# A new order for the last seven-product block, and its last output tile sent in quarters

One NeuronCore of one Trainium2 chip runs the kernel. The metric is device time in microseconds (us), the slowest core's; there is only one core here.

## The reference

A linear attention with decay over blocks of 64 tokens, followed by a two-layer perceptron with a tanh GELU. Cut to what matters:

```python
def _attn_setup():
    batch, n_heads, seq, head_dim = (4, 8, 768, 64)
...
    x = attn_out.transpose(0, 2, 1, 3).reshape(B * S, H * D)      # 3072 x 512
...
def _moe_ref(x, w_in, w_out):                                     # w_in 512 x 2048, w_out 2048 x 512
    h = x @ w_in
    c = np.float32(np.sqrt(2.0 / np.pi))
    g = 0.5 * h * (1.0 + np.tanh(c * (h + 0.044715 * h * h * h)))
    return (g @ w_out).astype(np.float32)
```

The change touches only the very last part of `g @ w_out`.

## The kernel before

The 3072 tokens are worked through in groups; from the third group on a group has 512 tokens. The second matrix product of such a group is done with seven block products in place of eight (a Strassen scheme). The tokens form two halves of 256 (T = 0, 1), the output columns two halves of 256 (e = 0, 1). A "pair" p is 128 tokens of the upper half together with 128 of the lower; a group has two pairs, and each pair takes seven products of 8 matmuls. The results land in PSUM banks called A to E, and VectorE combines them into an output tile `o` with four quarters `o[:, e, T, :]`. Quarters with e = T are the diagonal.

```python
        banks = {}
        PLACE = {4: ("A", 0), 3: ("A", 1), 5: ("B", 0), 2: ("B", 1), 1: ("C", 0), 7: ("D", 0),
                 6: ("D", 1)}

        def product(m, p):
            name, half = PLACE[m]
            final = g == len(groups) - 1 and p == HN // P - 1
            if final and m == 6:
                name = "E"
            ...                                   # 8 matmuls into banks[name][:, half]
            if m == 2:                            # A and B are complete
                o = banks["o"] = otp.tile([P, 2, 2, HE], FP32, tag="o32", name="o32")
                ...                               # ScalarE copies B to m525 (L476, L477)
                pin(tt(banks["diag"], A[:], m525[:, 0:2], ALU.subtract))        # L480
                pin(tt(flat[:, 1:3], A[:], m525[:, 1:3], ALU.add))              # L481: off-diagonal, final
            elif m == 1:
                d = banks["diag"]
                pin(tt(d, banks["C"][:, 0].unsqueeze(1).to_broadcast([P, 2, HE]), d, ALU.add))   # L484
            elif final and m in (7, 6):
                ...
                if m == 7:
                    low = row0 + HN + p * P
                    pin(nc.sync.dma_start(out=out[low : low + P, 0:HE], in_=o[:, 0, 1, :]))      # L492
                d = o[:, T, T, :]
                pin(tt(d, banks[name][:, half], d, ALU.add))                    # L494
                if m == 7:
                    pin(nc.scalar.dma_start(out=rows, in_=o[:, :, 0, :]))       # L496: 256 KB
                else:
                    pin(nc.sync.dma_start(out=rows[:, 1], in_=d))               # L498: 128 KB
            elif m == 6:                          # every other pair
                ...                               # L501, then two transfers of 256 KB (L504)
        ...
        for p in range(HN // P):
            for m in (3, 4, 5, 2, 1, 7, 6):
                filler.append(lambda m=m, p=p: product(m, p))
```

`pin` keeps program order. In the last group nothing else is left to run beside these products.

Of the kernel before, what the change touches and what calls it, by code (L numbers as in the profile page):

```python
# [15 lines left out]
def kernel(  # L16
# [10 lines left out]
    nc = tc.nc  # L27
    pin = tc.keep_in_program_order
    P = 128
# [47 lines left out]
    HF, HE = NF // 2, DM // 2  # L77
# [302 lines left out]
    groups = [[0, 1], [2], [3], [4, 5], [6, 7], [8, 9], [10, 11]]  # L380
    group_of = {sb: (g, i) for g, sbs in enumerate(groups) for i, sb in enumerate(sbs)}
    filler = []

    def queue_group(g):
# [22 lines left out]
        row0 = groups[g][0] * SB  # L407
# [19 lines left out]
        HN = N // 2  # L427
# [7 lines left out]
        def block(T, F, i):  # L435
            return gT[:, i, F, T * HN : (T + 1) * HN]
# [8 lines left out]
                i = slice(i0, i1)  # L445
                pin(nc.vector.tensor_tensor(gsum[m][:, i, :], block(T0, F0, i), block(T1, F1, i), op))  # L446

        banks = {}
        PLACE = {4: ("A", 0), 3: ("A", 1), 5: ("B", 0), 2: ("B", 1), 1: ("C", 0), 7: ("D", 0),
                 6: ("D", 1)}  # L450

        def product(m, p):

            name, half = PLACE[m]
            final = g == len(groups) - 1 and p == HN // P - 1
            if final and m == 6:
                name = "E"
            if m in (3, 5, 1, 7) or name == "E":
                banks[name] = ps_M.tile([P, 2, HE], FP32, tag="M", name=f"M{name}")
            dst = banks[name][:, half]  # L460
            t = slice(p * P, p * P + P)
            for i in range(HF):
                lhsT = block(*G_PLAIN[m], i)[:, t] if m in G_PLAIN else gsum[m][:, i, t]
                if m in W_PLAIN:
                    F, E = W_PLAIN[m]
                    rhs = w_out16[:, F * HF + i, E * HE : E * HE + HE]
                else:
                    rhs = w_sum16[:, w_slot[m], i, :]
                pin(nc.tensor.matmul(dst, lhsT, rhs, start=(i == 0), stop=(i == HF - 1),  # L469
                                     skip_group_check=True))  # L470
            tt = nc.vector.tensor_tensor
            if m == 2:
                o = banks["o"] = otp.tile([P, 2, 2, HE], FP32, tag="o32", name="o32")
                A, B = banks["A"], banks["B"]
                m525 = mtp.tile([P, 3, HE], FP32, tag="m525", name="m525")
                pin(nc.scalar.activation(out=m525[:, 0:2], in_=B[:], func=AF.Copy))  # L476
                pin(nc.scalar.activation(out=m525[:, 2], in_=B[:, 0], func=AF.Copy))  # L477
                flat = o[:].rearrange("p e t d -> p (e t) d")
                banks["diag"] = flat[:, 0:4:3]
                pin(tt(banks["diag"], A[:], m525[:, 0:2], ALU.subtract))  # L480
                pin(tt(flat[:, 1:3], A[:], m525[:, 1:3], ALU.add))  # L481
            elif m == 1:
                d = banks["diag"]
                pin(tt(d, banks["C"][:, 0].unsqueeze(1).to_broadcast([P, 2, HE]), d, ALU.add))  # L484
            elif final and m in (7, 6):

                o, T = banks["o"], (0 if m == 7 else 1)
                row = row0 + T * HN + p * P
                rows = out[row : row + P, :].rearrange("q (e d) -> q e d", e=2)
                if m == 7:  # L490
                    low = row0 + HN + p * P
                    pin(nc.sync.dma_start(out=out[low : low + P, 0:HE], in_=o[:, 0, 1, :]))  # L492
                d = o[:, T, T, :]
                pin(tt(d, banks[name][:, half], d, ALU.add))  # L494
                if m == 7:
                    pin(nc.scalar.dma_start(out=rows, in_=o[:, :, 0, :]))  # L496
                else:
                    pin(nc.sync.dma_start(out=rows[:, 1], in_=d))  # L498
            elif m == 6:
                d = banks["diag"]  # L500
                pin(tt(d, banks["D"][:], d, ALU.add))  # L501
                for T in range(2):
                    row = row0 + T * HN + p * P
                    pin(nc.sync.dma_start(out=out[row : row + P, :].rearrange("q (e d) -> q e d", e=2),  # L504
                                          in_=banks["o"][:, :, T, :]))
# [16 lines left out]
        if g == 0:  # L522
# [9 lines left out]
            order = [(tau, part) for part in (0, 2, 1, 3) for tau in range(3)]  # L532
# [7 lines left out]
        if g == 1:  # L540
# [1 line left out]
                for part in (0, 2, 1, 3):  # L542
                    filler.append(lambda tau=tau, part=part: mm2(tau, part))
            return
        for p in range(HN // P):
            for m in (3, 4, 5, 2, 1, 7, 6):
                filler.append(lambda m=m, p=p: product(m, p))

        def behind(k, i0, i1):

# [28 lines left out]
    def R(n, s):  # L579
        if n is not None:  # L580
            scores(n)
        products(n, s)
        if n is not None:
            causal(n)
        if s is not None and s % 2 == 1:
            g, i = group_of[s // 2]
            if i == len(groups[g]) - 1 and g > 0:
                queue_group(g)
        if n is not None:
            update(n, 0)  # L590
# [41 lines left out]
    banks = products(3, None)  # L632
# [3 lines left out]
    cast_win(0, 256, 512, 256, c01, on_act=True)  # L636
    causal(3)
    queue_group(0)
    fill(4)
    products(None, 3, banks)  # L640
# [46 lines left out]
    for n in range(8, NSTEP + 1):  # L687
        m = n if n < NSTEP else None
# [42 lines left out]
```

## Time and profile before

| | before |
|---|---|
| time, median of 3 (range) | 207.87 us (207.51 to 208.07) |
| span of the profiled run | 205.60 us |
| TensorE busy | 96% |
| products of the last group | 188.34 to 200.58 us |
| last addition on VectorE starts | 200.95 us |
| last output transfer issued / landed | 201.39 / 204.05 us |

The page of a profile gives busy shares and the chain of work that ended last. A line of the timeline reads: start and length in us, engine and line of code, operation, output and inputs, count; a bracket at its end tells how long the engine stood idle before it and what ended that. SPq and ACTq are the queues on which SyncE and ScalarE issue transfers: the length there is that of the issue, not of the transfer. When packets moved and when each transfer landed is in the trace's own records; those I quote in the text.

### The profile page before, as it was taken

To read this page: it belongs to the slowest core of one execution; us is meant where nothing else is said; L and a number is where in the kernel's file an instruction comes from. 1 tells how busy PE (TensorE), PEld (TensorE's weight loads), DVE (VectorE), ACT (ScalarE), POOL (GpSimd) and SP (SyncE) were. 2 spreads that over 40 slices of the span, in tenths; PEclk is the share of its full clock that TensorE was granted. 3 is DMA by queue.
4 is the path that set the end of the run, shared out by engine and by line. 5 is a ranking of instruction groups with operands and counts; after the bars stand their busy time and mean duration, and the time that the engine had idled before them with its cause. 6 is when DMAs were issued, how large, how long until landed. Compare 5 with 4: busy or idle time off the path is not lost.

```text
span 205.6 us, 5583 instructions
## 1 busy us (share of the span) xinstructions
PE 197.1 (96%) x2321; PEld 128.0 (62%) x2321; DVE 144.4 (70%) x271; ACT 108.1 (53%) x204; POOL 69.9 (34%) x80
## 2 busy tenths in 40 slices
PE   7988999999999999999999999999999999999990
PEld 2554644456875788644788554788555888446880
DVE  4788627867699998929997639996559474056631
ACT  2355778475882573487541577442676323665110
POOL 5495123646586851326224403404420110000000
PEclk9999999999999999999999999999999999999999
DMA  5999999999999998996549981736320003300033
GB/s 137 298 322 387 387 387 376 277 291 332 333 248 243 294 235 154 202 279 161 141 102 274 230 234 50 190 70 156 103 54 0 3 0 105 104 0 0 3 102 102
DMA packets 64057, 37.85 MB, mean 184 GB/s; under 512 B 17696, under 2 KB 59168, under 8 KB 64032
## 3 DMA queue, kind: packets, MB, share of 16 engines
q1 hardware_dynamic: 63760, 37.24, 66.9%
q8 instruction: 18, 0.29, 0.6%
q10 hardware_dynamic: 272, 0.26, 0.4%
q14 instruction: 7, 0.06, 0.1%
HBM read 27.27 MB, written 6.29 MB: 163 GB/s over the span
## 4 chain that ended last, share of the span: by engine, by line
PE 91%; DVE 2%; DMA 2%; issue 1%; ACT 1%; DVEq 0%
PE Hps L401 35%; PE O2ps L416 10%; PE MB L469 8%; PE MA L469 7%; PE MD L469 7%; PE Sps L271 4%; PE MC L469 4%; PE Hps L514 4%; PE OK L329 3%; PE idle L573 3%; PE OK L320 3%; PE Tps L242 2%; DMA qkT<-qk 2%; PE OK L306 1%; DVE t L366 1%
## 5 line engine op out<-in xcount | busy, mean ns | idle before, releaser
L401 PE MATMUL Hps<-xT,w_in 128*128 128x512 f16 (+1 forms) x416 | 79.1, 346 | 0.0
L405 ACT ACTIVATE gT<-Hps 128x512 f16<-128x512 f32 x88 | 52.3, 597 | 22.6 <-PE Hps L401 21.8
L401 PEld LDWEIGHTS <-w_in 128*128 128x128 f16 x416 | 40.2, 98 | 33.5
L373 POOL TENSOR_TENSOR u<-t,lumask 128x256 f16<-128x256 f32 x40 | 31.4, 791 | 80.9 <-DVE t L366 54.2
L446 DVE TENSOR_TENSOR gs<-gT 128x512 f16<-128x512 f16 (+1 forms) x70 | 36.6, 586 | 10.8 <-ACT gT L405 10.6
L280 DVE TENSOR_TENSOR PT<-Sps,mask 128x1024 f16<-128x1024 f32 x24 | 29.2, 1217 | 17.3 <-PE Sps L271 17.2
L469 PEld LDWEIGHTS <-gs 128*128 128x128 f16 x360 | 34.9, 98 | 4.0
L211 POOL TENSOR_TENSOR v<-v,dv 128x512 f16<-128x512 f32 x24 | 29.2, 1219 | 4.7 <-DMA v<-in_v_dram 4.7
L343 ACT ACTIVATE xT<-OK 128x256 f16<-128x256 f32 x48 | 18.2, 453 | 20.0 <-PE OK L329 16.5
L416 PE MATMUL O2ps<-w_out,gT 128*128 128x512 f16 x96 | 21.9, 379 | 0.0
L476 ACT ACTIVATE m<-MB 128x512 f32<-128x512 f32 x9 | 5.4, 597 | 28.1 <-PE MB L469 28.1
L226 ACT ACTIVATE qk<-k 128x512 f16<-128x512 f32 x24 | 15.0, 624 | 8.8 <-DMA k<-in_k_dram 8.8
L221 DVE TENSOR_TENSOR qk<-q,dq 128x512 f16<-128x512 f32 x23 | 19.2, 834 | 0.0
L469 PE MATMUL MA<-w_sum,gT 128*128 128x256 f16 x144 | 17.5, 273 | 0.1
L469 PE MATMUL MD<-w_sum,gs 128*128 128x256 f16 x136 | 17.5, 273 | 0.0
L469 PE MATMUL MB<-w_out,gs 128*128 128x256 f16 x144 | 17.2, 273 | 0.0
L366 DVE SCALAR_TENSOR_TENSOR t<-t,lamu,OK 128x64 f32<-128x64 f32 x64 | 14.5, 273 | 2.1 <-PE OK L306 0.9
L480 DVE TENSOR_TENSOR o<-MA,m 128x512 f32<-128x512 f32 x9 | 6.2, 688 | 13.9 <-ACT m L476 13.9
L469 PEld LDWEIGHTS <-gT 128*128 128x128 f16 x144 | 14.0, 98 | 2.8 <-ACT gT L405 0.3
L416 PEld LDWEIGHTS <-gT 128*128 128x128 f16 x96 | 9.2, 98 | 9.9
L271 PEld LDWEIGHTS <-qkT 64*64 64x64 f16 x384 | 6.1, 106 | 8.3 <-issue 4.2
L123 DVE TENSOR_TENSOR w_sum<-wo,wo 128x1024 f16<-128x1024 f32 x6 | 7.9, 1362 | 4.2 <-DMA wo<-in_moe_w_out_dram 4.2
(55 smaller groups left out, 169.2 us busy)
## 6 DMA issues: line engine op xcount, KB each, us to landing
q<-in_q_dram SPq DMA_DIRECT2D x24, 256.0 KB, 4.5
k<-in_k_dram SPq DMA_DIRECT2D x24, 256.0 KB, 5.0
v<-in_v_dram SPq DMA_DIRECT2D x24, 256.0 KB, 4.9
out_dram<-o SPq DMA_DIRECT2D x22, 256.0 KB, 3.4
wo<-in_moe_w_out_dram SPq DMA_DIRECT2D x4, 1024.0 KB, 9.2
wi<-in_moe_w_in_dram SPq DMA_DIRECT2D x4, 512.0 KB, 8.0
wi<-in_moe_w_in_dram SPq DMA_DIRECT2D x2, 1024.0 KB, 12.5
out_dram<-o SPq DMA_DIRECT2D x2, 128.0 KB, 2.2
```

What stands on the lines that cost most here:

```text
L211: pin(nc.gpsimd.tensor_tensor(wide(tv[:]), ld32[s][2][:], decay(dv, s), ALU.mult))
L221: pin(q_eng.tensor_tensor(wide(tq), q32[:], decay(dq, s), ALU.mult))
L226: pin(nc.scalar.activation(out=wide(tk), in_=k32[:], func=AF.Copy))
L280: pin(nc.vector.tensor_tensor(t[:].rearrange("p a b c d -> p (a b) (c d)"), Ss.pop(n)[:].rearrange("p a b c d -> p (a b) (c d)"), mask[:]. ...
L343: pin(nc.scalar.activation(out=dst[:, :, c * P : (c + 1) * P].rearrange("p hp (t j) -> p hp j t", j=2), in_=OK[c][:, 0:256].rearrange("p ( ...
L366: pin(nc.vector.scalar_tensor_tensor(t[:, hp, :], state[half][:, hp, :], lamu[:, 2 * half + hp : 2 * half + hp + 1], K[:, hp, :], ALU.mult ...
L373: pin(nc.gpsimd.tensor_tensor(u[:], state[half][:].unsqueeze(2).to_broadcast([P, 2, 2, D]), lumask[:, 2 * half : 2 * half + 2, :].unsqueez ...
L401: pin(nc.tensor.matmul(by_block(Hps[:, i, :]), w_in16[:, c, f * P : (f + 1) * P], x(c), start=(c == 0), stop=(c == NC - 1)))
L405: pin(nc.scalar.activation(out=dst, in_=Hps[:], func=AF.Gelu_apprx_tanh))
L416: pin(nc.tensor.matmul(O2[tau][0][:], gT[:, f % HF, f // HF, tau * P : (tau + 1) * P], w_out16[:, f, :], start=(n == 0), stop=(n == NF - 1)))
L446: pin(nc.vector.tensor_tensor(gsum[m][:, i, :], block(T0, F0, i), block(T1, F1, i), op))
L469: pin(nc.tensor.matmul(dst, lhsT, rhs, start=(i == 0), stop=(i == HF - 1), skip_group_check=True))
```

## The change

Intent: in the last group the first four products of both pairs run first, then the other three of each. So the long part of the second pair's combination (ScalarE's copy, L480, L481) lies beside matmuls instead of behind the last ones. And the second pair's tile leaves in quarters as they become final, on two queues, so that little is left at the end.

```diff
-        banks = {}
+        of_pair = {}
...
+            banks = of_pair.setdefault(p, {})
...
                 pin(tt(flat[:, 1:3], A[:], m525[:, 1:3], ALU.add))
+                if final:
+                    for T, queue in ((1, nc.sync), (0, nc.scalar)):
+                        row = row0 + T * HN + p * P
+                        E = slice((1 - T) * HE, (1 - T) * HE + HE)
+                        pin(queue.dma_start(out=out[row : row + P, E], in_=o[:, 1 - T, T, :]))
...
-                if m == 7:
-                    low = row0 + HN + p * P
-                    pin(nc.sync.dma_start(out=out[low : low + P, 0:HE], in_=o[:, 0, 1, :]))
                 d = o[:, T, T, :]
                 pin(tt(d, banks[name][:, half], d, ALU.add))
-                if m == 7:
-                    pin(nc.scalar.dma_start(out=rows, in_=o[:, :, 0, :]))
-                else:
-                    pin(nc.sync.dma_start(out=rows[:, 1], in_=d))
+                queue = nc.scalar if m == 7 else nc.sync
+                pin(queue.dma_start(out=rows[:, T], in_=d))
...
-        for p in range(HN // P):
-            for m in (3, 4, 5, 2, 1, 7, 6):
-                filler.append(lambda m=m, p=p: product(m, p))
+        ms = ((3, 4, 5, 2), (1, 7, 6))
+        order = [(m, p) for p in range(HN // P) for m in ms[0] + ms[1]]
+        if g == len(groups) - 1:
+            order = [(m, p) for part in ms for p in range(HN // P) for m in part]
+        for m, p in order:
+            filler.append(lambda m=m, p=p: product(m, p))
```

## The prediction

> **What bounds the kernel now.** I read the page first: the busy line of TensorE and the shares of the chain that ended last.
>
> ```profile
> PE 197.1 (96%) x2321; PEld 128.0 (62%) x2321; DVE 144.4 (70%) x271; ACT 108.1 (53%) x204; POOL 69.9 (34%) x80
> ...
> PE 91%; DVE 2%; DMA 2%; issue 1%; ACT 1%; DVEq 0%
> ```
>
> TensorE is busy for 96% of a span of 205.6 us, and 91% of the last chain is TensorE. The change neither adds nor removes a matmul: it orders the 14 products of the last group anew. So it can only act on what follows the last matmul. Next, the chain in order of time, at its end.
>
> ```profile
> 188.34 1.75 PE MA L469 x16
> 190.09 1.75 PE MB L469 x16
> 191.84 0.87 PE MC L469 x8
> 192.71 1.75 PE MD L469 x16
> 194.46 1.75 PE MA L469 x16
> 196.20 1.75 PE MB L469 x16
> 197.95 0.87 PE MC L469 x8
> 198.82 0.87 PE MD L469 x8
> 199.69 0.89 PE ME L469 x8
> 200.61 0.42 DVE o L494
> ```
>
> A product is 8 matmuls and takes 0.87 us. The 14 products run from 188.34 to 200.58 without a gap, so TensorE can end no sooner. From there to the end of the span are 5.02 us; they are the whole stake. The timeline of the other engines over that stretch:
>
> ```profile
> 197.99 0.60 ACT L476 ACTIVATE m<-MB 128x512 f32<-128x512 f32 x1 [5.24 <-PE MB L469]
> ...
> 198.61 0.69 DVE L480 TENSOR_TENSOR o<-MA,m 128x512 f32<-128x512 f32 x1 [3.43 <-ACT m L476]
> ...
> 199.82 0.68 DVE L484 TENSOR_TENSOR o<-MC,o 128x512 f32<-128x512 f32 x1
> 199.93 0.38 SPq L492 DMA_DIRECT2D out_dram<-o  x1
> 200.61 0.42 DVE L494 TENSOR_TENSOR o<-MD,o 128x256 f32<-128x256 f32 x1
> 200.95 0.41 DVE L494 TENSOR_TENSOR o<-ME,o 128x256 f32<-128x256 f32 x1
> 201.06 0.64 ACTq L496 DMA_DIRECT2D out_dram<-o  x1
> 201.39 0.36 SPq L498 DMA_DIRECT2D out_dram<-o  x1
> ```
>
> Here VectorE, not TensorE, sets the end. Product MB of the second pair ends at 197.95; the copy by ScalarE and five dependent VectorE operations follow one behind the other: 197.99, 198.61, 199.22 (left out above), 199.82, 200.61, 200.95. Product MD was ready at 199.69, but its addition began at 200.61; ME was ready at 200.58, but its addition began at 200.95. The chain names ME as what released the addition of MD. I don't follow it there: by the code that addition needs MD alone, and it starts 0.79 us after L484, whose result it reads. In the first pair L501 also starts 0.78 after its L484 (193.71 to 194.49); there its product ended 0.03 before, so the two causes can't be told apart, and 0.79 is an upper bound for the dependent step.
>
> Last, the landings. The DMA view, cut to the issues at 199.93 and at 201.39 in turn, gives:
>
> ```profile
> out_dram<-o SPq DMA_DIRECT2D x1, 128.0 KB, 1.7
> ```
>
> ```profile
> out_dram<-o ACTq DMA_DIRECT2D x1, 256.0 KB, 2.8
> out_dram<-o SPq DMA_DIRECT2D x1, 128.0 KB, 2.7
> ```
>
> The same 128 KB on the same queue landed after 1.73 us when alone (last landing 201.66 in the trace's records), and after 2.66 us (204.05) when issued 0.33 us behind the 256 KB of ScalarE's queue (203.89). The packet records say why: alone, first packet at 200.8, 0.9 after issue; the second time, 1.5 after issue, while the other queue's packets already ran from 202.3. From the last landing to the end of the span are 205.60 - 204.05 = 1.55 us of closing semaphores, which I take as constant.
>
> **What the Trainium skill says.** (1) "DMA: Bandwidth & Descriptors", "Anatomy of one DMA": a fixed cost near 2 us per DMA, most of it the wait for the write to be confirmed, plus bytes over bandwidth (the section is on the software path). Of the lone transfer's 1.73 us, 0.9 lay ahead of the first packet, about 0.45 were packets and some 0.35 the confirmation: fixed cost dominates as it says, but its larger part here is before the data. (2) The same page, "Issuing engines are not separate DMA queues": all queues run on the same 16 DMA engines and interleave, so a second one only saves issue time. The trace agrees: from 202.9 both queues share some 340 GB/s. (3) "Perfetto Trace Analysis", "DMA Instruction — HWDGE (DVE, Sync)": descriptor generation is a block shared by two sequencers (drawn for VectorE and SyncE, with a note that SyncE and ScalarE work the same way), locked for exclusive use. That fits the late first packet of the last transfer (0.6 us more than the lone one, and the other's issue took 0.64), though no run here isolates it. (4) "VectorE: DVE Perf Modes", "The DRAIN you can't avoid": a same-engine read-after-write needs a semaphore. That fits 0.79 between L484 and L494 where independent operations start 0.61 apart.
>
> **The change part by part.** *Order.* The second pair's MB ends after 8 products: 188.34 + 7.0 = 195.33 in place of 197.95. ScalarE's copy then starts at 195.37 and VectorE's two operations at 195.99 and 196.60, ended by 197.28. This moves 2.6 us of chain beside matmuls. First pair: its L484 follows at 197.20; its product MD ends at 197.95, so L501 runs 197.98 to 198.67. Second pair: MC ends 198.82, so L484 is at 198.85; MD ends 199.69, so its addition is at 199.72 (the dependent step would allow 199.64); ME ends 200.58, its addition starts at 200.61. That is 0.34 us before the old 200.95, and now TensorE sets it. The counts of matmuls, copies and VectorE operations are unchanged.
>
> *Transfers.* The two off-diagonal quarters of the second pair leave at about 197.3, one per queue, 128 KB each, landing before 199.5: hidden. The first pair's two 256 KB move from 195.21 to 198.70 (0.72 from L501's start to issue before; the same taken). Before, they took from 195.21 to 198.41 to land; 3.2 us later than 198.70 is 201.90, their packets about 199.9 to 201.5. MD's quarter on ScalarE's queue leaves at 199.72 + 0.45 = 200.17 with 128 KB in place of 256, and shares bandwidth with them until roughly 201.9. The last quarter leaves at 200.61 + 0.44 = 201.05. No issue lies just ahead of it: ScalarE's should end at about 200.17 + 0.37 = 200.54. So I give it the lone transfer's 1.73: landed at 202.78, against 204.05.
>
> *Sum.* 0.34 from VectorE and 2.66 - 1.73 = 0.93 from the last transfer: 1.27 us. Span 202.78 + 1.55 = 204.33; time 207.87 - 1.27 = 206.60. I keep back 0.15 for the first pair's 512 KB, now close to the end: **206.75 us**.
>
> **The rivals.** *The last transfer is held up anyway.* The 512 KB now go out 3.5 us later, so packets and descriptors of three transfers crowd 199.9 to 201.9. If the last quarter again needs 2.66 from issue, only 0.34 is gained: 207.53. For it: the case above. Against it: the first packet is due at 201.05 + 0.9 = 201.95, when by my sums the others have ended. *A new wait takes the place of the old.* L484 of the second pair now writes the diagonal of tile o while two transfers read its other quarters. Were the regions kept apart only coarsely, L484 would wait for landings at about 199.3, MD's addition would move to 200.1, but ME's could still start at 200.61: at most some tenths. Against it: before, the transfer at 201.39 was issued though the one at 199.93, to the other columns of the same rows, had not landed until 201.66, so interleaved regions are told apart at least there. *TensorE stalls on banks.* Six PSUM banks now hold A, B of both pairs and C, D of the first; the seventh tile (197.95) needs the first bank, last read by L481 of the first pair near 193.8: 4 us of slack. The one-buffer copy tile m525 is wanted at 195.37 and also free at 193.8. A stall would cost its full length, but I see none. *It was hidden anyway.* If the closing 1.55 us were held by something other than the landing, nothing would move: 207.9. Against it: the SyncE queue's longest wait at the end, 2.3 us, is for an output transfer.
>
> **Range and chances.** The full sum gives 206.6, the first rival 207.5. Single times before range from 207.51 to 208.07, so 0.3 either way comes from scatter. Range 206.1 to 207.6. Faster by over 2% means under 203.8, 4.1 us of the 5.02 after the last matmul, of which the transfer and closing alone take 3.3: 0.005. Slower by over 2% would need 4 us of new stall: 0.01. Within 2%: 0.985.
>
> **What the changed profile should show.** The chain: products in the order A, B, A, B, C, D, C, D, E to 200.6 without a gap. VectorE: the last addition released by ME, within 0.05 us of its end, not queued behind MD's. The last issue on SyncE's queue at about 201.05, landing after 1.7 to 2.0 us; a span of about 204.4. The prediction is wrong if that transfer again takes 2.7 us, if L484 of the second pair starts later than 198.9 with a transfer as its releaser, or if a gap opens between the products.

## The result

The changed kernel took 206.11 us (median of 4, 205.95 to 206.34); the kernel before, run beside it, 207.69 us. The ratio is 0.9924, with a 95% interval of 0.9903 to 0.9945. Ratios here are the mean time of one kernel's fast runs over that of the other's of the same rounds, so not quite the ratio of the medians. In the profiled runs the span went from 205.60 to 204.33 us.

The chain that ended last, of the changed kernel, in order of time (the code has moved: L470 is the old L469):

```profile
188.30 1.75 PE MA L470 x16
190.05 1.75 PE MB L470 x16
191.79 1.75 PE MA L470 x16
193.54 1.75 PE MB L470 x16
195.28 0.87 PE MC L470 x8
...
199.65 0.89 PE ME L470 x8
200.56 0.42 DVE o L497
```

The products stand in the new order A, B, A, B, C without a gap, start to end in the same 12.2 us as before. The last addition now starts right at the end of ME. The timeline of the other engines (all lines of matmuls and weight loads left out):

```profile
195.32 0.60 ACT L477 ACTIVATE m<-MB 128x512 f32<-128x512 f32 x1 [2.62 <-PE MB L470]
...
195.95 0.69 DVE L481 TENSOR_TENSOR o<-MA,m 128x512 f32<-128x512 f32 x1 [2.21 <-ACT m L477]
...
197.16 0.68 DVE L490 TENSOR_TENSOR o<-MC,o 128x512 f32<-128x512 f32 x1
197.27 0.38 SPq L487 DMA_DIRECT2D out_dram<-o  x1
197.27 0.39 ACTq L487 DMA_DIRECT2D out_dram<-o  x1
...
198.66 1.21 SPq L505 DMA_DIRECT2D out_dram<-o  x2
198.82 0.69 DVE L490 TENSOR_TENSOR o<-MC,o 128x512 f32<-128x512 f32 x1 [0.18 <-PE MC L470]
...
199.69 0.42 DVE L497 TENSOR_TENSOR o<-MD,o 128x256 f32<-128x256 f32 x1 [0.18 <-PE MD L470]
200.15 0.34 ACTq L499 DMA_DIRECT2D out_dram<-o  x1
200.56 0.42 DVE L497 TENSOR_TENSOR o<-ME,o 128x256 f32<-128x256 f32 x1 [0.45 <-PE ME L470]
201.01 0.36 SPq L499 DMA_DIRECT2D out_dram<-o  x1
```

Before, no bracket stood at the two last additions: VectorE came to them late and never waited. Now each of the last three operations waits for its product (idle 0.18, 0.18 and 0.45 us), so VectorE follows TensorE. The last issue moved from 201.39 to 201.01. The DMA view, cut to that issue:

```profile
out_dram<-o SPq DMA_DIRECT2D x1, 128.0 KB, 1.7
```

It landed 1.74 us after its issue, at 202.76, in place of 2.66 us, at 204.05.

### The profile page after: what moved, and what is told of

It is laid out like the page before. It is cut to its first block, busy times and chain, and to the rows that moved or that the text cites. A ratio compares the mean times of both kernels' runs of the same rounds, so it can differ in the third digit from the quotient of the medians.

```text
span 204.3 us, 5584 instructions
## 1 busy us (share of the span) xinstructions
PE 196.8 (96%) x2321; PEld 127.6 (62%) x2321; DVE 144.8 (71%) x271; ACT 107.7 (53%) x204; POOL 70.1 (34%) x80
## 4 chain that ended last, share of the span: by engine, by line
PE 89%; DMA 3%; SPq 2%; ACT 1%; DVE 1%; issue 1%
PE Hps L401 37%; PE O2ps L416 10%; PE MB L470 8%; PE MA L470 7%; PE MD L470 7%; PE Sps L271 4%; PE MC L470 4%; PE Hps L515 4%; PE OK L329 3%; PE OK L320 3%; DMA k<-in_k_dram 3%; SPq L68 2%; PE OK L306 1%; PE Tps L242 1%; DVE t L366 1%
## 5 line engine op out<-in xcount | busy, mean ns | idle before, releaser
L470 PEld LDWEIGHTS <-gs 128*128 128x128 f16 x360 | 34.9, 98 | 4.0
L470 PE MATMUL MA<-w_sum,gT 128*128 128x256 f16 x144 | 17.5, 273 | 0.1
L470 PE MATMUL MD<-w_sum,gs 128*128 128x256 f16 x136 | 17.5, 273 | 0.0
L470 PE MATMUL MB<-w_out,gs 128*128 128x256 f16 x144 | 17.2, 273 | 0.0
L470 PEld LDWEIGHTS <-gT 128*128 128x128 f16 x144 | 14.0, 98 | 2.8 <-ACT gT L405 0.3
L481 DVE TENSOR_TENSOR o<-MA,m 128x512 f32<-128x512 f32 x9 | 6.2, 688 | 12.3 <-ACT m L477 12.3
```

Source lines behind the costliest of these rows:

```text
L470: pin(nc.tensor.matmul(dst, lhsT, rhs, start=(i == 0), stop=(i == HF - 1), skip_group_check=True))
```

## The experiments

The start-up of this kernel moves the whole trace by some tenths of a microsecond from run to run: the last matmul starts anywhere from 200.15 to 200.88 us in the traces used below (E7 excepted), more than most effects asked about. So the table counts from the start of the last matmul to the end of the span. Three profiles of the changed kernel gave 4.08, 4.07 and 4.09 us for this stretch; measured like that, a tenth of a microsecond can be read. Each other kernel has one profile.

| kernel | last addition starts | last issue | issue to last landing | closing | whole stretch |
|---|---|---|---|---|---|
| before | 0.65 | 1.09 | 2.66 | 1.55 | 5.31 |
| changed | 0.31 | 0.76 | 1.74 | 1.57 | 4.08 |
| E1 order alone | 0.31 | 0.76 | 2.40 | 1.12 | 4.29 |
| E2 transfers alone | 0.65 | 1.09 | 1.77 | 1.57 | 4.44 |
| E3 before, one queue | 0.65 | 1.40 | 2.23 | 1.49 | 5.12 |
| E4 before, 2 KB pieces | 0.71 | 1.16 | 2.14 | 1.55 | 4.84 |
| E5, E11 changed again | 0.31 | 0.76 | 1.75 | 1.56, 1.57 | 4.07, 4.09 |
| E6 changed, one queue | 0.31 | 0.76 | 1.74 | 1.47 | 3.97 |
| E7 last quarter by rows | 0.31 | 0.77 | 2.24 | 1.58 | 4.58 |
| E8 last quarter by columns | 0.52 | 0.83 | 1.68 | 1.52 | 4.02 |
| E9 early quarters on ScalarE | 0.31 | 0.76 | 1.75 | 1.32 | 3.84 |
| E10 first pair on two queues | 0.31 | 0.76 | 1.75 | 1.15 | 3.66 |

The columns are us; "closing" runs from the last landing to the end of the span. The first two give moments counted from the last matmul's start; the third begins at the issue. From "before" to "changed" the 1.23 us are 0.33 of the earlier last issue (VectorE's step is 0.34) and 0.92 of the last transfer, less 0.02 of closing.

Two theories stood for the 0.92 us. **A**, the prediction's: the last transfer was late because ScalarE's issue lay 0.33 us ahead of it and the descriptors are made one after the other. **B**: the transfer engines move some 340 GB/s; what is still unsent near the end sets the last landing, whoever issued it and when.

### E1: the order alone

```diff
 (the kernel before)
-        for p in range(HN // P):
-            for m in (3, 4, 5, 2, 1, 7, 6):
+        (the changed kernel's order and banks per pair; the transfers stay as they were)
```

> The kernel before with the new order of products alone; the transfers stay as they were (one early quarter, then 256 KB on ScalarE's queue, then the last quarter). Theory A (the prediction as written: VectorE's step 0.34 us, and the last transfer was late because ScalarE's issue lay just ahead of it): ScalarE's issue now starts near 200.15 and ends before the last one at 201.0, so the last lands after 1.7 to 1.9 us, at about 202.8, and nearly all of the 1.3 us is gained. Theory B (bytes: what is still to be sent near the end sets the landing): 1 MB has to leave between 199.85 and the end at some 345 GB/s, last packets at about 202.8, last landing 203.2 to 203.4, gain about 0.8 us. Both: the last addition on VectorE starts at 200.56 to 200.61.

Measured: ratio to the kernel before 0.9955 (0.9939 to 0.9972), 206.42 against 207.38 us. The last addition came as early as in the changed kernel. ScalarE's issue ran from 200.50 to 201.14, over 0.23 us before the last one began at 201.37; yet that last one took:

```profile
out_dram<-o SPq DMA_DIRECT2D x1, 128.0 KB, 2.4
```

So nothing lay just ahead, and still it was late: against theory A. The view of E1 by stretches (stretch, length, busy time of the five engines, granted clock, DMA share, GB/s) shows why:

```profile
201.00:201.50 0.50, 0.00 (x0) 0.00 (x0) 0.35 (x1) 0.00 (x0) 0.00 (x0) 1.00 1.06 346
201.50:202.00 0.50, 0.00 (x0) 0.00 (x0) 0.00 (x0) 0.00 (x0) 0.00 (x0) 1.00 1.04 340
202.00:202.50 0.50, 0.00 (x0) 0.00 (x0) 0.00 (x0) 0.00 (x0) 0.00 (x0) 1.00 1.03 346
202.50:203.00 0.50, 0.00 (x0) 0.00 (x0) 0.00 (x0) 0.00 (x0) 0.00 (x0) 1.00 0.97 340
```

All other engines are done and the transfer engines are full. From 200.2 to 203.4 they moved 1 MB without a pause: the first pair's 512 KB, now late because of the order, the early quarter queued behind them, the 256 KB and the last quarter. A had said that nearly all of the 1.3 us would be gained, B about 0.8; counted from the last matmul the landing is at 3.16 in place of 3.75 us, 0.6 sooner. The time gained more than that, 0.9 us, because the closing was 0.43 us shorter; E9 and E10 take that up.

### E2: the transfers alone

```diff
 (the changed kernel)
-        if g == len(groups) - 1:
-            order = [(m, p) for part in ms for p in range(HN // P) for m in part]
```

> The changed kernel with the old order of products, so the transfers in quarters alone. VectorE's last addition stays at 200.95, last issue at 201.39. Theory A: ScalarE's issue ahead of it now has half the descriptors (0.37 us in place of 0.64), so the hold is about halved: landing about 2.1 us after issue, at 203.5, gain 0.5 to 0.6. Theory B: 256 KB in place of 384 KB from a first packet near 201.95, last packets 202.7, landing 203.1 to 203.2, gain 0.85 to 0.95.

Measured: ratio 0.9957 (0.9941 to 0.9973), 206.54 us. ScalarE's issue still lay 0.33 us ahead of the last (201.38 and 201.71), as before the change, but with 128 KB:

```profile
out_dram<-o ACTq DMA_DIRECT2D x1, 128.0 KB, 1.8
out_dram<-o SPq DMA_DIRECT2D x1, 128.0 KB, 1.8
```

The last transfer took 1.77 us, almost as long as one alone. A had said 2.1, B a gain of 0.85 to 0.95; the stretch is 0.87 us shorter. As worded before the run, A missed and B held. But E2 alone does not part them: ScalarE's issue ended 0.01 us after the last one began (0.31 us before the change), so an A that counts only this overlap would have named about 1.75 too. It is E1 that speaks against A. And E2 halves the bytes of ScalarE's transfer together with the number of its pieces (contiguous rows of 1 KB, here 128 in place of 256); E4 parts these. E2 does size the parts of the change. The quarters alone are worth 0.89 us of the landing; the order alone 0.33 of the last issue and 0.26 of the transfer, 0.59 in all; both together 1.25. They overlap in 0.23: with the quarters in place, the order is worth the VectorE step and hardly more.

### E3: before, all on one queue

```diff
-                    pin(nc.scalar.dma_start(out=rows, in_=o[:, :, 0, :]))
+                    pin(nc.sync.dma_start(out=rows, in_=o[:, :, 0, :]))
```

> The kernel before with the 256 KB transfer of the last tile on SyncE's queue too, so all output on one queue. Theory A and B alike: the last landing stays within 0.2 us of 204.05, since the engines that carry the bytes are shared; the second queue saves nothing there. Rival C (the second queue is worth its issue time): SyncE issues 0.64 and then 0.36 us one after the other, last issue near 201.7 in place of 201.39, landing 204.4 or later, slower by 0.3 to 0.4 us.

Measured: 207.35 against 207.38 us, ratio 0.9994 (0.9975 to 1.0012). The last issue was 0.31 us later, the last landing 3.63 in place of 3.75 us after the last matmul's start. Rival C falls: the second queue saved issue time, and the landing did not follow the issue. Theories A and B agree here, so this run doesn't part them.

### E4: before, the 256 KB in pieces of 2 KB

```diff
-                o = banks["o"] = otp.tile([P, 2, 2, HE], FP32, tag="o32", name="o32")
+                o32 = otp.tile(...)              # the last pair: [token half][column half]
+                o = banks["o"] = o32[:].rearrange("p t e d -> p e t d") if last_pair else o32
...
-                    pin(nc.scalar.dma_start(out=rows, in_=o[:, :, 0, :]))
+                    pin(nc.scalar.dma_start(out=out[row : row + P, :], in_=(both quarters of T = 0 as one row)))
```

> The kernel before with the last pair's output tile laid out so that the 256 KB transfer goes as 128 pieces of 2 KB in place of 256 pieces of 1 KB; same bytes, half the descriptors; one more VectorE operation (two of 256 columns in place of one of 512, some 0.1 us later). Theory A (issue and descriptor generation hold the last transfer): ScalarE's issue takes 0.37, the last transfer's first packet comes 0.3 us nearer to its issue, 1.2 in place of 1.5. Theory B (bytes): the 256 KB start nearer to their issue (0.9 in place of 1.3 us), the 384 KB still take 1.1 us from there, last landing about 1.1 + 0.5 us after the first packet, so 0.2 to 0.3 us earlier than before in all. A rival in which a queue's packets are served in turns of a fixed number of descriptors: the last transfer's first packet stays 1.5 us behind its issue or comes later, since each turn now carries twice the bytes.

Measured: 207.04 us, ratio 0.9988 (0.9965 to 1.001): the timing doesn't resolve it. In the trace ScalarE's issue took 0.37 in place of 0.64 us, and its first packet came 0.9 us after the issue's start in place of 1.3. From there the 384 KB took 1.2 us (1.3 before), and the last landing came 0.46 us sooner, counted from the last matmul's start. The last transfer's own first packet came 1.2 us after its issue, which A had named; the landing came somewhat sooner than B's 0.2 to 0.3. So this run does not part the two. The third rival's 1.5 us or more were not seen, but the 256 KB were all but sent by then (their packets ended at 202.8, its own began at 202.6), so turns as long as a whole transfer are not excluded. What it adds: the time to the first packet went with the number of pieces, at the same bytes.

The DMA view, cut to the last two issues:

```profile
out_dram<-o ACTq DMA_DIRECT2D x1, 256.0 KB, 2.1
out_dram<-o SPq DMA_DIRECT2D x1, 128.0 KB, 2.1
```

Put between the kernel before and E2, this run divides what the two theories left mixed. Counted from the last matmul's start, the last landing came at 3.75 us before, at 3.29 with half the pieces and the same bytes (E4), and at 2.86 with half the bytes too (E2). So of the 0.89 us that the quarters are worth, 0.46 came with fewer pieces, since the transfer ahead of the last began 0.4 us nearer to its issue, and 0.43 with fewer bytes. B as worded above names the bytes alone; in its forecast for E4 it did count 0.2 to 0.3 us of an earlier start. This rests on one trace each of E4 and E2; in the three traces of the changed kernel the last landing, counted like this, differs by 0.01 us. The times of E4 don't resolve it.

### E5 and E11: the changed kernel again

They are the yardsticks of their calls, unaltered.

> The changed kernel once more, as the yardstick of this call. Ratio to the kernel before 0.992 to 0.994, last landing 2.2 us after the last matmul, closing 1.55 us.

> The changed kernel, as the yardstick of this call: closing 1.55 us, last landing 2.2 us after the last matmul, ratio to the kernel before 0.992 to 0.994.

Measured: 206.09 us, ratio 0.9921 (0.9897 to 0.9946), and 206.31 us, ratio 0.9957 (0.9939 to 0.9975; one of its six runs took 207.50). The second ratio lies outside what I had written; without that run it would be about 0.995, outside still. Why is not known: by medians the gain was 1.58 us beside the first measurement, 1.72 in E5's call and 1.05 in E11's, while the traces of the changed kernel agree to 0.02 us.

### E6: the changed kernel on one queue

```diff
-                    for T, queue in ((1, nc.sync), (0, nc.scalar)):
+                    for T, queue in ((1, nc.sync), (0, nc.sync)):
...
-                queue = nc.scalar if m == 7 else nc.sync
+                queue = nc.sync
```

> The changed kernel with all its quarters on SyncE's queue. Theory B (bytes still to be sent set the landing; the queue does not matter): the issues at 197.3 (two of 0.37), 198.7 (two of 0.6), 200.15 and 201.0 do not meet, so nothing moves: last landing within 0.15 us of the changed kernel's, ratio the same within 0.1%. Rival C (the second queue is part of the gain): the last transfer lands 0.3 us later or more.

Measured: 206.29 us, ratio 0.9937 (0.9909 to 0.9965); the last transfer landed 1.74 us after its issue, as with two queues. The ratio differs from E5's by 0.0016 where 0.001 was expected, but the intervals overlap and one run took 207.41. "On two queues" is no part of the gain that the trace shows.

### E7: the last quarter cut by rows

```diff
+                    for queue, r in ((nc.sync, slice(0, 64)), (nc.scalar, slice(64, 128))):
+                        pin(queue.dma_start(out=rows[r, T], in_=d[r]))
```

> The changed kernel with the last quarter cut by rows, 64 rows on each queue at the same time. Theory B plus generators that work side by side: half the descriptors per queue, each issue 0.2 us in place of 0.36, first packet 0.15 us sooner, last landing 0.1 to 0.2 us sooner, ratio to the changed kernel about 0.999. Theory A (one generator for both queues): the second half's first packet comes 0.2 us after the first's, no gain.

No gain, as A had said, and the second half's first packet came 0.29 us after the first's, where A had named 0.2. But neither theory had what follows. 207.25 us, ratio 0.997 (0.9942 to 0.9999). The DMA view, cut to these two issues:

```profile
out_dram<-o SPq DMA_DIRECT2D x1, 64.0 KB, 2.0
out_dram<-o ACTq DMA_DIRECT2D x1, 64.0 KB, 2.2
```

Half the bytes took longer: the issues took 0.52 and 0.55 us in place of 0.36, the first packets came 1.2 and 1.5 us after the issues in place of 0.9, and a packet of 1 KB took 65 ns on average in place of 47. Why 64 rows are slower is open. The stretch is 0.5 us longer than the changed kernel's; the other 0.6 us of the time lie elsewhere. In the profiled run TensorE fell back 1.05 us while the output weights were loading, at 26 to 44 us. That run was the slowest of its six, and whether the edit or chance did that isn't settled.

### E8: the last quarter cut by columns

```diff
+                    for queue, e in ((nc.scalar, slice(0, HE // 2)), (nc.sync, slice(HE // 2, HE))):
+                        pin(tt(d[:, e], banks[name][:, half, e], d[:, e], ALU.add))
+                        pin(queue.dma_start(out=rows[:, T, e], in_=d[:, e]))
```

> The changed kernel with the last addition and the last quarter cut by columns: 128 columns on ScalarE's queue, then 128 on SyncE's. The second addition starts 0.2 to 0.25 us after the first and ends at about the time of the one it replaces, so the last issue stays near 201.05; half the bytes are left for it, so its packets (512 B each) take some 0.2 us in place of 0.4. Theory B: last landing 0.1 to 0.2 us sooner. Theory A: the issue of the first half, 0.2 us ahead, holds the second, landing the same or up to 0.2 us later.

Measured: 206.34 us, ratio 0.9928 (0.9903 to 0.9953). The second addition of 128 columns took 0.29 us, where 256 columns took 0.42, so the last issue came 0.06 us later. The last landing came 1.68 us after it: no gain, 2.50 in place of 2.51 after the last matmul's start. B's 0.1 to 0.2 did not show; "the same" is what A had named. Yet the hold by which A explained it isn't there: the last transfer's first packet came 0.91 us after its issue, in the changed kernel 0.89, though ScalarE's issue ran on for 0.15 us beside it.

### E9 and E10: one transfer fewer on SyncE

E1's short closing asked for a cause. In every trace SyncE stands still for 0.35 to 0.40 us ahead of the 208th instruction that the trace records for it. In most kernels this falls among the closing semaphores, where all engines wait for SyncE; in E1, with one SyncE instruction fewer, it falls one place later. Two ways to take one transfer from SyncE:

```diff
 E9
-                    for T, queue in ((1, nc.sync), (0, nc.scalar)):
+                    for T, queue in ((1, nc.scalar), (0, nc.scalar)):
 E10 (the first pair's two transfers of 256 KB)
-                    pin(nc.sync.dma_start(out=...
+                    last = g == len(groups) - 1 and T == 1
+                    queue = nc.scalar if last else nc.sync
+                    pin(queue.dma_start(out=...
```

> The changed kernel with both early quarters on ScalarE's queue, so SyncE has one transfer fewer to issue. In every trace so far SyncE pauses for 0.35 to 0.38 us ahead of the 208th of its recorded instructions; in all kernels but the order alone this falls among the closing semaphores, between the last landing and the end, where all wait for SyncE. The order alone has 210 SyncE instructions in place of 211, its pause falls one place later, where nobody waits, and its closing took 1.13 us in place of 1.55. If that is the cause, this kernel's closing is 1.15 to 1.2 us, span 203.9 to 204.3 by the start-up's scatter, and the time 0.3 to 0.4 us under the changed kernel's. If the pause isn't tied to the count, closing stays at 1.55 and nothing moves. The last landing stays 2.2 us after the last matmul either way.

> The changed kernel with the first pair's second 256 KB on ScalarE's queue. It too takes one transfer from SyncE, so the closing should be 1.15 to 1.2 us as well if the count is the cause. ScalarE issues it at about 198.7 to 199.3, well before its quarter at 200.15, and 512 KB still leave between 199.9 and 201.4: last landing unmoved within 0.1 us.

Measured: E9 206.15 us, ratio 0.9937 (0.9924 to 0.995), 209 SyncE instructions, closing 1.32 us: a fall of 0.25 us in place of about 0.4, since the pause fell ahead of a later drain that was waited for too. Its median is 0.16 us under the changed kernel's of the same call (0.3 to 0.4 expected). E10 206.02 us, ratio 0.9946 (0.9919 to 0.9974), 210 instructions, closing 1.15 us as expected, and the shortest stretch of all, 3.66 us. The pause stayed at the 208th instruction in both, so it is tied to the count. By medians E10 beats the changed kernel of the same call by 0.29 us, but the intervals overlap (E10 has one run of 207.94), so only the trace shows the gain. A like pause of 0.44 to 0.46 us stands ahead of the 80th instruction, 128 places earlier, in every trace. The two would fit the borders of blocks of instructions, but that the pause is a fetch stays an inference: the trace's instruction queue shows no packet during the closing pause in any run, and one of 8 KB 0.6 to 0.9 us after its end, which the record assigns to no engine.

## Why the prediction was right, and where not

- **The bound.** Right. TensorE's products took the same 12.2 us, and all of the gain lies behind them.
- **The order: 0.34 us on VectorE.** Right, to the hundredth: the last addition starts 0.31 in place of 0.65 us after the last matmul's start. E1 shows it without the quarters, E2 its absence with them.
- **The last transfer: 0.93 us.** The size was right (0.92), the reason was wrong in the main. The step that failed reads "No issue lies just ahead of it", and with it the reading that the other transfer's issue had held the last one. In E1 no issue lay just ahead, its first packet still came 1.5 us after its issue, and it took 2.40 us. In the changed trace the two issues at 197.27 ran at once, 0.38 and 0.39 us long, and their first packets came 0.12 us apart: if a shared generator made the second wait, it cost about 0.1 us (0.3 in E7). What counted was the transfer sent beside the last one: half the pieces, so that its own packets began 0.4 us sooner (E4), and half the bytes (E2). So the number of pieces did count, as the prediction's reading of descriptor generation would have it, but through the other transfer's own start and not through a lock. The lone transfer's 1.73 held because by then, as the prediction did say in its first rival, the others had ended: their packets ran to 201.92, its own from 201.90. So the size came out right on that working, not on the reason given for the hold: where the others had not ended (E1), that reason missed the landing by 0.5 to 0.7 us.
- **The 0.15 us kept back** for the first pair's late 512 KB were not needed. They landed at 201.91, as worked out (201.90).
- **The closing.** Constant to 0.02 us between the two kernels, but not constant in general: 1.12 to 1.58 us over the runs, by where SyncE's pause falls.
- **The rivals.** The last transfer was not held up again. L484 of the second pair (now L490) was released by MC at 198.82, not by a landing. No bank stall appeared.
- **The total.** The sum of 1.27 us was met in the span, 205.60 to 204.33, with 0.04 of it from the start-up: after the last matmul's start it was 1.23. The time of 206.11 lies in the range by 0.01 us, which is luck: the medians fell by 1.58 us, more than the traces show. The prediction started from a median of 207.87 and gave back 0.15; 207.69 was measured beside the change, and the ratio's interval (1.1 to 2.0 us) holds 1.27.
- **The chain's last link.** The prediction did not follow the profile where it named ME as what released MD's addition. In the changed kernel that addition starts at 199.69, before ME ends, so it needs no ME. E4 shows the rest: its VectorE work ran 0.06 us later, and MD's addition started 0.78 us after its L484 (there L491), as before, but 0.09 us behind ME's end in place of 0.03; the chain of that trace names L491. So the 0.79 us are the dependent step.
- **Small slips.** "Five dependent VectorE operations" are not all dependent: L481 writes other quarters than L480 and L484, and the two additions of L494 do not read each other. A fall of 2% from 207.87 ends at 203.7, not 203.8. Nothing rests on either.

## What to carry to other kernels

When one engine is full to the end, count what stands behind its last instruction: the work of other engines that could have run beside it, and the bytes that are still unsent. Move both forward, and let what is sent near the end consist of few pieces (E4). Which queue issues the bytes mattered little here (E3, E6), and a later issue with less to send landed before an earlier one with more (E2 issued 0.33 us later than E1, counted from the last matmul, and landed 0.30 us sooner). Measure such tails from the last instruction of the full engine, since the start-up's scatter is larger than they are.

## What the Trainium skill lacked or had wrong

- "DMA: Bandwidth & Descriptors", "Anatomy of one DMA", puts most of the fixed cost in the confirmation of the write (for the software path). For these transfers from SBUF to HBM on the hardware queues the larger part lay ahead of the first packet: about 0.85 us from issue for 128 pieces and 1.2 to 1.3 for 256, against some 0.4 us from the last packets to the landing. The section calls the making of descriptors a small part; here 256 pieces took 0.4 us longer to the first packet than 128 pieces of the same 256 KB (E4: 0.9 us in place of 1.3).
- "Perfetto Trace Analysis", "DMA Instruction — HWDGE (DVE, Sync)", draws a generator that is locked for exclusive use. Two issues from SyncE and ScalarE at the same moment (197.27) took 0.38 and 0.39 us, hardly longer than one alone (0.36 to 0.38), so no lock shows in these issue times. It isn't ruled out: their first packets came 0.12 us apart, and in E7 two issues of 64 rows at the same moment took 0.52 and 0.55 us, with no lone one to compare.
- "Runtime: NRT & Kernel Launch", "Instruction fetch mechanics", calls the cost of crossing a block of instructions mostly hidden. If SyncE's pause is that, it was 0.35 to 0.40 us here, always ahead of the same recorded instruction, and in plain sight when it fell into the closing (1.55 against 1.15 us).
- No page has that two transfers of 64 rows, issued at once on two queues, can be slower than one of 128 rows: 2.0 and 2.2 us for 64 KB each (E7) against 1.7 for 128 KB.
